# Transformed convolution with batch norm: loads as whole 128-row arrays, and a new order of the first jobs, products and weights

## The chip, the core and the metric

The kernel runs on one core of a Trainium2 chip. A core has a matrix engine (TensorE, PE in the profile; PEld is its weight load), a vector engine (VectorE, DVE), a scalar engine (ScalarE, ACT), a general engine (GpSimd, POOL) and a queue engine (SyncE, SP) that issues most DMA transfers. The memory beside the engines has 128 partitions; matrix products land in PSUM, which has 8 banks here called 0 to 7, and PE may write a bank again only when its last reader is done. The metric is the device time of one execution in microseconds (us), given as the median of several.

## The reference

A one-dimensional convolution with 3 taps over a sequence, then batch norm with given mean and variance, then SiLU. Batch is 2, sequence length 2048, 1024 channels in and out, all in bf16:

```python
xp = jnp.pad(x, ((0, 0), (P, P), (0, 0)))            # P = 1
y = sum(jnp.einsum('bsc,cd->bsd', xp[:, k:k + S, :], w[k]) for k in range(3))
inv_std = 1.0 / jnp.sqrt(var + 1e-5)
y = (y - mean) * (g * inv_std) + b
return jax.nn.silu(y)
```

## The kernel before

The convolution is done in a transformed domain: six outputs at a time come from eight products instead of eighteen. The sequence is cut into groups of six rows, 342 of them, each read as a window of eight rows. The work has four steps.

**Jobs: transform of x.** A load of x (`load_x`, L106) brings one batch (of 2) and one block of 128 input channels (of 8): 128 partitions, 16 windows of 128 rows; there are 16 such loads, of 512 KB. A job matmul (L241) multiplies one window, as stationary operand, with the matrix `rm`, which holds the eight points for 21 groups: 168 columns. 6, 6 and then 4 such matmuls make one job, so that a load of x gives three jobs and all of it 48 jobs and 256 matmuls. A job fills two banks, and ACT (L264) or DVE (L266) cast it to bf16 into `T_sb`. The last six groups of each batch are a "short" block: one load `xl` (L102) of 48 rows, eight small matmuls (L255), one cast.

**Weights.** For each block of 128 output channels (`dc`, 8 of them) the three taps W0, W2, W1 (in this order in memory) become eight transformed weights. Products 0 and 7 use W0 and W2 as they are; for the six others POOL makes a sum `e` (L134) for each of three pairs, out of multiples of the taps (POOL L126 or ACT L124), and from each sum two weights `u` (L147), by adding and subtracting W1 or its double. The first block's are made by `FirstWeights`: W0 and W2 are loaded first, W1 later, and steps are issued in a fixed order as soon as their inputs have been issued. Multiples named in the order string (`m2a`: multiple 2 on ACT) are made there, the others on POOL. The second block is made by `prepare_second`, later ones by `prepare_w`.

**Units: products and their combination.** A unit is one output block and one batch: eight products of eight matmuls (342 columns each, over the input blocks), in four banks, with copies, combinations on DVE (L309) and SiLU on ACT (L313). There are 16 units. In the first, products are issued one matmul at a time (L414): "ends" are products 0 and 7, which go to banks 2 and 3 and are copied out into `kept`; "p" are products 1 to 6. Later units use L294.

**Parameters.** `scales` on POOL (L216 to L225) turns variance, gain, mean and offset (`prm`) into a scale and an offset per output channel. It stands ahead of the first weights on POOL.

**What sets the order.** All engine queues are written out by hand, each engine runs its instructions in order, and SP's queue holds the loads in the order of the program: three loads of x, the short block, W0 and W2, the other loads of x (L106; each needs a free one of six buffers), W1, the second batch, its short block, the second block of weights. `rm` and `prm` go on ACT's queue. While x is transformed, the string `ORDER` says what PE does next: a letter A to D is one job, into banks 4, 6, 2 or 0 and the bank behind it, with `a`, `d` for the engine that casts it (two letters: one for each bank); `s2d` is a short block into bank 2, cast by DVE; a number is so many end products, `p` and a number so many of products 1 to 6; `+` is one waiting combination; `m2a` a multiple. Before it, PE runs three warm-up products on zeros (L87).

Of the kernel before, what the change touches and what calls it, by code (L numbers as in the profile page):

```python
# [8 lines left out]
ALU = mybir.AluOpType  # L9
FP32 = mybir.dt.float32  # L10
BF16 = mybir.dt.bfloat16
ENG = mybir.EngineType

P = 128
R = 6
NJ = 8
WT = 21
XBUFS = 6
LROWS = 48
SROW = 66  # L20
# [6 lines left out]

BANKS = {"A": 4, "B": 6, "C": 2, "D": 0}
ORDER = (
    "Bad Aad Da Cda Bda Ad Da Bda s2d Aad Dad Bad 2 Aa Dda 1 Bda Aad 1 Dad 1 Bda 1 Aa 1 Dda 1 Bda 1 Ada "  # L30
    "Dda Bad 1 m2a 2 Dd 2 Bda Aad Dda 2 Bad Aad p4 Ca p1 Bad p2 Aad Cda Ba p1 Ada p2 Ca p1 Bda p2 Aad p1 "
    "Ca p1 Bda p1 Aa p1 Cd p2 Bad p5 + Cad Ba p4 s4a Ca Bda Aa"
)

W0, W2, W1 = range(3)
COPIES = {0: "a", 7: "d", 1: "d", 3: "d", 2: "a", 5: "a"}

@with_exitstack
def kernel(
# [2 lines left out]
    x: bass.AP,  # L42
    xl: bass.AP,
    w: bass.AP,
    prm_in: bass.AP,
    rm_in: bass.AP,
    out: bass.AP,
):
    nc = tc.nc
    B, CT, _, NF, _ = x.shape  # L50
    DC = w.shape[0]
    NB = NTILES
    LAST = NB - NF * WT
# [22 lines left out]
    T_sb = [tpool.tile([P, CT, NJ, NB], BF16, name=f"T_sb{bi}") for bi in range(B)]  # L76


    rm = consts.tile([P, NJ, WT], BF16, name="rm")
    nc.scalar.dma_start(out=rm, in_=rm_in)  # L80
    prm = consts.tile([P, 4, DC], BF16, name="prm")


    zero = consts.tile([P, 1], FP32, name="zero")
    nc.gpsimd.memset(zero, 0.0)
    for n in (384, 384, 216):
        nc.tensor.matmul(  # L87
            ps[:, 3, 0:n], lhsT=zero.broadcast_to([P, P]), rhs=zero.broadcast_to([P, n]), start=True, stop=True,
        )
    zeros = consts.tile([P, 64], FP32, name="zeros")  # L90
    nc.vector.memset(zeros, 0.0)
# [12 lines left out]
    def load_x(bi, ct):  # L104
        xt[bi, ct] = t = xpool.tile([P, NF, P], BF16, name="xw")
# [26 lines left out]
    def even(dc, q, a, b):  # L132
        sums[dc, q] = epool.tile([P, CT, P], FP32, name=f"e{q}")
        nc.gpsimd.tensor_tensor(sums[dc, q], a, b, op=ALU.add)  # L134
# [29 lines left out]
    class FirstWeights:  # L164
# [3 lines left out]
        def __init__(self, dc):  # L168
            w0, w2 = raw[dc][:, W0], raw[dc][:, W2]
            self.dc, self.src, self.made = dc, ((w2, 4.0), (w0, 4.0), (raw[dc][:, W1], 2.0)), {}  # L170
            elsewhere = [int(t[1]) for t in ORDER.split() if t[0] == "m"]
            self.steps = [(None, lambda: even(dc, 0, w0, w2))]
            self.steps += [(i, lambda i=i: self.multiple(i, nc.gpsimd)) for i in (0,) if i not in elsewhere]
            self.steps += [(0, lambda: even(dc, 1, self.made[0], w0))]
            self.steps += [(i, lambda i=i: self.multiple(i, nc.gpsimd)) for i in (1,) if i not in elsewhere]
            self.steps += [(1, lambda: even(dc, 2, self.made[1], w2))]
            self.steps += [(i, lambda i=i: self.multiple(i, nc.gpsimd)) for i in (2,) if i not in elsewhere]
            self.steps += [
                (2 if q else None, lambda q=q, i=i: transform_w(dc, q, (i,)))
                for q, i in ((0, 0), (1, 0), (0, 1), (1, 1), (2, 0), (2, 1))  # L180
            ]
# [32 lines left out]
    beta = consts.tile([P, DC], FP32, name="beta")  # L214

    def scales():  # L216
        mhalf = consts.tile([P, DC], FP32, name="mhalf")
        nc.gpsimd.memset(mhalf, -0.5)
        sc = consts.tile([P, DC], FP32, name="sc")
        nc.gpsimd.tensor_scalar(sc, prm[:, 0, :], 1e-5, 1.0, op0=ALU.add, op1=ALU.mult)  # L220
        nc.gpsimd.tensor_tensor(sc, sc, mhalf, op=ALU.pow)
# [3 lines left out]
        nc.gpsimd.tensor_scalar(scale, sc, 1.0 / 36.0, 0.0, op0=ALU.mult, op1=ALU.add)  # L225
# [3 lines left out]
    class Jobs:  # L229
# [20 lines left out]
        def do_short(self, bank, eng):  # L250
            bi = self.short.pop(0)
            src = ps[:, bank, 0:CT * NJ * LAST].rearrange("p (c j n) -> p c j n", j=NJ, n=LAST)
            rows, n = (slice(0, P), SROW // R) if bi else (slice(0, LROWS), 0)
            for c in range(CT):
                nc.tensor.matmul(  # L255
                    src[:, c], lhsT=small[rows, c * P:(c + 1) * P], rhs=rm[rows, :, n:n + LAST],
                    start=True, stop=True,
                )
            dst = T_sb[bi][:, :, :, NT:NB].rearrange("p c j n -> p (c j) n")
            self.out(dst, src.rearrange("p c j n -> p (c j) n"), eng)  # L260
# [127 lines left out]
    class First(Unit):  # L388
# [3 lines left out]
        def __init__(self, dc, bi):  # L392
            super().__init__(dc, bi, 0)
            self.sd = dpool.tile([P, 4, NB], FP32, name="sd")
            self.t = [
                consts.tile([P, 2, NB], FP32, name="f0"), ypool2.tile([P, 2, NB], FP32, name="t1"),
                consts.tile([P, 2, NB], FP32, name="f2"),
            ]
            self.kept = consts.tile([P, 2, NB], FP32, name="kept")
            self.ends = [(j, q, False, ct) for ct in range(CT) for j, q in ((0, 2), (NJ - 1, 3))]  # L400
            self.todo = [
                (j, q, add, ct) for j, q, add in (
                    (1, 1, False), (3, 0, False), (2, 1, True), (4, 0, True), (5, 2, False), (6, 2, True),
                ) for ct in range(CT)
            ]
            self.p, self.later = {}, []
# [128 lines left out]

    nc.scalar.dma_start(out=prm, in_=prm_in)
    for ct in range(3):
        load_x(0, ct)  # L540
    load_small(0)
    load_w(0, slice(W0, W1))
    scales()
    nc.scalar.activation(dummy[:, 1:2], dummy[:, 0:1], ACT.Silu)
    for ct in range(3, CT):
        load_x(0, ct)
    load_w(0, slice(W1, W1 + 1))
    for ct in range(CT):
        load_x(1, ct)
    load_small(1)  # L550
# [7 lines left out]
    for token in ORDER.split():  # L558
# [49 lines left out]
    inner, outer = slice(2, R), slice(0, 2)  # L608
    h0 = Half(dc, bi, 4, 0)

    nc.tensor.matmul(ps[:, 5, 0:H], lhsT=zeros[:, 0:64].bitcast(BF16), rhs=T_sb[bi][:, 0, 0, 0:H], start=True, stop=True)  # L611
    h0.run(quiet, prev.rest(quiet, 5, 5))
    prev.store(nc.sync)
    h1 = Half(dc, bi, 0, 1)
# [21 lines left out]
def _laid_out(np, x, w, mean, var, g, b):  # L636


    B, S, C = x.shape
    K, _, D = w.shape  # L640
    CT, DC = C // P, D // P
    NF = S // (R * WT)
    step = R * WT
    xp = np.zeros((B, step * NF + P, C), x.dtype)
    xp[:, 1:S + 1] = x
    wins = np.stack([xp[:, f * step:f * step + P] for f in range(NF)], 2)
    wins = wins.reshape(B, P, NF, CT, P).transpose(0, 3, 1, 2, 4)
# [40 lines left out]
```

## Time and profile before

| | |
|---|---|
| median of 3 runs | 180.94 us (180.89 to 181.15) |
| profiled execution | 180.88 us, its span 179.1 us |
| PE busy | 172.7 us, 96% of the span |
| POOL busy | 139.7 us, 78% |
| DVE busy | 147.6 us, 82% |
| ACT busy | 110.2 us, 62% |
| chain that ended last | PE 86%, DMA 8%, DVE 3%, ACT 1% |
| DMA | 24.58 MB, mean 137 GB/s over the span |

The chain is followed back from the last instruction. Its DMA share, 8%, lies in the first 19 us, where x comes in; from there to about 170 us it is PE alone, and at the end the last unit's combinations and stores. So the table of averages says little on the head, and the prediction reads that part in order of time. In rows of the trace, a start and a length are in us from the start of the span; a bracket gives the idle time of the engine before it and what ended that; x and a number count instructions that the row merges.

### The profile page before, as it was taken

What the parts mean: (1) busy time and instruction counts of PE and PEld (TensorE: products, weight loads), DVE (VectorE), ACT (ScalarE), POOL (GpSimd) and SP (SyncE); (2) the same over time, 40 slices, a digit from 0 to 9 for tenths busy, and PEclk for the clock granted to TensorE, in tenths of its full rate; (3) what the DMA queues carried; (4) which work ended last, traced back from release to release, by engine and by line L of the source; (5) the groups of instructions that cost most, each with busy time, mean ns of one, the idle gap of its engine ahead of it and who ended that gap; (6) DMA issues with size and microseconds to landing.
All of it is one profiled execution on the core that took longest, in us unless ns stands there. A gap on an engine that the chain in (4) does not pass through costs nothing.

```text
span 179.1 us, 3534 instructions
## 1 busy us (share of the span) xinstructions
PE 172.7 (96%) x1367; PEld 123.5 (69%) x1367; DVE 147.6 (82%) x211; ACT 110.2 (62%) x191; POOL 139.7 (78%) x77
## 2 busy tenths in 40 slices
PE   8879999999999999999999999999999999999991
PEld 4869888766666666666666666666666666668891
DVE  1779998897969999997878788898979987766691
ACT  3779999959374837374636654565356554563774
POOL 2599999999997799999999999999799959000000
PEclk9999999999999999999999999999999999999999
DMA  5999993450344031813082306330303030203033
GB/s 187 374 410 404 410 383 124 129 226 0 132 141 170 0 132 8 260 45 132 0 221 90 134 0 168 143 134 0 135 0 132 0 130 6 98 34 132 3 149 117
DMA packets 6912, 24.58 MB, mean 137 GB/s; under 512 B 1040, under 2 KB 1552, under 8 KB 6896
## 3 DMA queue, kind: packets, MB, share of 16 engines
q1 hardware_dynamic: 6464, 24.25, 36.8%
q8 instruction: 10, 0.16, 0.3%
q10 hardware_dynamic: 432, 0.12, 0.3%
q14 instruction: 6, 0.05, 0.1%
HBM read 14.93 MB, written 9.44 MB: 136 GB/s over the span
## 4 chain that ended last, share of the span: by engine, by line
PE 86%; DMA 8%; DVE 3%; ACT 1%; SPq 0%; issue 0%; DVEq 0%
PE ps L294 75%; DMA xw<-in_x_dram 8%; PE ps L241 6%; PE ps L414 4%; DVE ps L309 2%; DVE t L309 1%; ACT yh L313 1%; SPq L106 0%; PE ps L255 0%; DVEq L677 0%; DVE sd L309 0%; PE ps L611 0%; DVEq L309 0%
## 5 line engine op out<-in xcount | busy, mean ns | idle before, releaser
L294 PE MATMUL ps<-T_sb,u 128*128 128x342 bf16 (+2 forms) x768 | 109.4, 298 | 0.0
L294 PEld LDWEIGHTS <-u 128*128 128x128 bf16 x768 | 72.3, 97 | 32.6
L147 POOL TENSOR_TENSOR u<-e,w1x 128x1024 bf16<-128x1024 f32 x32 | 71.5, 2258 | 6.1 <-DVE e L140 6.0
L294 PE MATMUL ps<-T_sb,wch 128*128 128x342 bf16 (+2 forms) x256 | 39.5, 299 | 0.4 <-DVE ps L309 0.4
L309 DVE SCALAR_TENSOR_TENSOR t<-ps,sd 128x684 f32<-128x684 f32 (+2 forms) x49 | 37.6, 819 | 0.5
L313 ACT ACTIVATE yT<-ps,beta,scale 128x342 bf16<-128x342 f32 (+1 forms) x42 | 29.2, 727 | 12.6 <-PE ps L294 12.6
L147 POOL TENSOR_TENSOR u<-e,wch 128x1024 bf16<-128x1024 f32 x16 | 35.7, 2251 | 0.5
L294 PEld LDWEIGHTS <-wch 128*128 128x128 bf16 x256 | 24.2, 97 | 11.1 <-issue 0.5
L303 ACT COPY pc<-ps 128x342 f32<-128x342 f32 (+2 forms) x32 | 13.6, 425 | 27.9 <-PE ps L294 27.0
L266 DVE CAST T_sb<-ps 128x504 bf16<-128x504 f32 (+3 forms) x37 | 22.8, 664 | 6.8 <-PE ps L241 6.3
L264 ACT CAST T_sb<-ps 128x504 bf16<-128x504 f32 (+4 forms) x46 | 25.5, 640 | 3.7 <-PE ps L241 3.6
L309 DVE SCALAR_TENSOR_TENSOR ps<-ps,t 128x684 f32<-128x684 f32 (+2 forms) x32 | 26.5, 829 | 0.7
L309 DVE SCALAR_TENSOR_TENSOR ps<-ps,pc 128x342 f32<-128x342 f32 (+2 forms) x34 | 16.9, 498 | 11.5 <-PE ps L294 8.8
L241 PE MATMUL ps<-rm,xw 128*128 128x168 bf16 x256 | 23.2, 236 | 1.8 <-DMA xw<-in_x_dram 1.6
L241 PEld LDWEIGHTS <-xw 128*128 128x128 bf16 x256 | 19.7, 98 | 4.8 <-DMA xw<-in_x_dram 2.9
L140 DVE SCALAR_TENSOR_TENSOR e<-wch 128x1024 f32<-128x1024 bf16 x12 | 21.0, 1749 | 0.0
L134 POOL TENSOR_TENSOR e<-wch 128x1024 f32<-128x1024 bf16 x8 | 19.0, 2374 | 0.1
L313 ACT ACTIVATE yT<-t,beta,scale 128x684 bf16<-128x684 f32 x15 | 14.4, 958 | 0.0
L309 DVE SCALAR_TENSOR_TENSOR sd<-pc,ps 128x342 f32<-128x342 f32 (+2 forms) x17 | 8.2, 485 | 7.4 <-ACT sd L303 7.4
L309 DVE SCALAR_TENSOR_TENSOR t<-ps,t 128x684 f32<-128x684 f32 (+2 forms) x17 | 13.9, 817 | 0.0
L303 ACT COPY sd<-ps 128x342 f32<-128x342 f32 (+2 forms) x16 | 6.8, 428 | 10.6 <-PE ps L294 8.9
L305 ACT ACTIVATE pc<-ps 128x342 f32<-128x342 f32 (+2 forms) x16 | 7.0, 438 | 8.7 <-PE ps L294 6.0
(44 smaller groups left out, 68.2 us busy)
## 6 DMA issues: line engine op xcount, KB each, us to landing
out_dram<-yT SPq DMA_DIRECT2D x15, 576.0 KB, 2.8
xw<-in_x_dram SPq DMA_DIRECT2D x16, 512.0 KB, 7.2
wch<-in_w_dram SPq DMA_DIRECT2D x7, 768.0 KB, 5.5
wch<-in_w_dram SPq DMA_DIRECT2D x1, 512.0 KB, 6.5
wch<-in_w_dram SPq DMA_DIRECT2D x1, 256.0 KB, 8.5
out_dram<-yh SPq DMA_DIRECT2D x1, 256.0 KB, 2.1
xl<-in_xl_dram SPq DMA_DIRECT2D x2, 96.0 KB, 5.9
out_dram<-yh SPq DMA_DIRECT2D x1, 128.0 KB, 1.7
```

Source lines behind the costliest of these rows:

```text
L134: nc.gpsimd.tensor_tensor(sums[dc, q], a, b, op=ALU.add)
L140: nc.vector.scalar_tensor_tensor(out=e, in0=f, scalar=4.0, in1=h, op0=ALU.mult, op1=ALU.add)
L147: nc.gpsimd.tensor_tensor(wts[dc, q][:, i], sums[dc, q], o, op=(ALU.add, ALU.subtract)[i])
L241: nc.tensor.matmul(src[:, q // per, q % per], lhsT=xt[bi, ct][:, f + q], rhs=rm, start=True, stop=True)
L264: nc.scalar.copy(dst, src)
L266: nc.vector.tensor_copy(dst, src)
L294: nc.tensor.matmul(self.bank[q], lhsT=lhsT, rhs=T_sb[self.bi][:, ct, j, nsl], start=not add and ct == 0, stop=ct == CT - 1, skip_group_che ...
L303: nc.scalar.copy(dst, self.bank[q])
L305: nc.scalar.mul(dst, self.bank[q], by)
L309: nc.vector.scalar_tensor_tensor(out=out, in0=in0, scalar=scalar, in1=in1, op0=ALU.mult, op1=op1)
L313: nc.scalar.activation(self.yT[:, rows, self.y0:self.y0 + self.hi - self.lo], src, ACT.Silu, bias=beta[:, dc:dc + 1], scale=scale[:, dc:dc ...
L414: nc.tensor.matmul(self.bank[q], lhsT=lhsT, rhs=T_sb[self.bi][:, ct, j, :], start=not add and ct == 0, stop=ct == CT - 1, skip_group_check ...
```

## The change

- `rm`, a copy of it for the short blocks, and `prm` become one array `head` with 128 rows, loaded in one transfer on ACT's queue.
- The short block of a batch is laid out by the host as 128 rows and three columns of 128 channels: three blocks of 40 rows stand above each other in a column, and the matrix for them is zero outside the 40 rows of its block. `small` becomes one tile for each batch, of 128 rows; the clearing of it goes. The eight short matmuls of a batch stay.
- W1 is loaded behind the fifth load of x instead of the eighth.
- `FirstWeights`: the two weights of a sum follow that sum, instead of all six behind the three sums. Multiple 1 goes to ACT (`m1a`); multiple 0 stays on POOL.
- The first unit's products run 1, 2, 3, 4, 5, 6 instead of 1, 3, 2, 4, 5, 6; one of its combinations goes (another takes its value from a neighbour), `kept` shares a tile with a result, and the copies of products 0 and 7 change engines.
- `ORDER` is another, with the first products ahead of the third load's last job.
- The warm-up is 24 columns shorter; the zero operands and -0.5 are taken from other tiles.

```diff
-LROWS = 48
-SROW = 66
+LROWS = 40
+STACK = 3
 ORDER = (
-    "Bad Aad Da Cda Bda Ad Da Bda s2d Aad Dad Bad 2 Aa Dda 1 Bda Aad 1 Dad 1 Bda 1 Aa 1 Dda 1 Bda 1 Ada "
-    "Dda Bad 1 m2a 2 Dd 2 Bda Aad Dda 2 Bad Aad p4 Ca p1 Bad p2 Aad Cda Ba p1 Ada p2 Ca p1 Bda p2 Aad p1 "
-    "Ca p1 Bda p1 Aa p1 Cd p2 Bad p5 + Cad Ba p4 s4a Ca Bda Aa"
+    "Dad Bad Aa Cda Bda Dd Aad s2a Ba 1 Dd 1 m1a 2 Aad Dad 1 Ba Ada 1 Dda 1 Bd 1 m2a Dda Ada 2 Bad Dda "
+    "Aad 2 Ba p5 Ada Bda p1 1 Ada p1 1 Bda 2 p1 Aad Ba Cda p4 Ada p1 Cad p3 + + Aad + p3 Ca p2 Bda p1 "
+    "Ada p2 Cad Ba Ada p2 Cda p1 Bda Ada Cda Bda p2 Aad p1 s3a Bda Ada Cda p1 Ba Aa"
 )
+COPIES = {0: "d", 7: "a", 1: "d", 3: "d", 2: "a", 5: "a"}
-COPIES = {0: "a", 7: "d", 1: "d", 3: "d", 2: "a", 5: "a"}
...
-    rm = consts.tile([P, NJ, WT], BF16, name="rm")
-    nc.scalar.dma_start(out=rm, in_=rm_in)
-    prm = consts.tile([P, 4, DC], BF16, name="prm")
+    ends = (0, NJ * WT, NJ * (WT + STACK * LAST))
+    first = consts.tile([P, head.shape[1]], BF16, name="head")
+    nc.scalar.dma_start(out=first, in_=head)
+    rm = first[:, :ends[1]].rearrange("p (j n) -> p j n", j=NJ)
+    rm_short = first[:, ends[1]:ends[2]].rearrange("p (s j n) -> p s j n", s=STACK, j=NJ)
+    prm = first[:, ends[2]:].rearrange("p (i d) -> p i d", i=4)
...
-    for n in (384, 384, 216):
+    for n in (384, 384, 192):
...
-    small = xlpool.tile([P, CT * P], BF16, name="xl")
-    nc.vector.memset(small, 0.0)
+    small = [xlpool.tile([P, xl.shape[2]], BF16, name=f"xl{bi}") for bi in range(B)]
     def load_small(bi):
-        nc.sync.dma_start(out=small[bi * SROW:bi * SROW + LROWS], in_=xl[bi])
+        nc.sync.dma_start(out=small[bi], in_=xl[bi])
...
-            self.steps = [(None, lambda: even(dc, 0, w0, w2))]
-            self.steps += [(i, lambda i=i: self.multiple(i, nc.gpsimd)) for i in (0,) if i not in elsewhere]
-            self.steps += [(0, lambda: even(dc, 1, self.made[0], w0))]
...
-                for q, i in ((0, 0), (1, 0), (0, 1), (1, 1), (2, 0), (2, 1))
-            ]
+            self.steps = [(None, lambda: even(dc, 0, w0, w2))] + weights(0)
+            self.steps += multiple(0) + [(0, lambda: even(dc, 1, self.made[0], w0))] + multiple(2) + weights(1)
+            self.steps += multiple(1) + [(1, lambda: even(dc, 2, self.made[1], w2))] + weights(2)
...
-                    src[:, c], lhsT=small[rows, c * P:(c + 1) * P], rhs=rm[rows, :, n:n + LAST],
+                    src[:, c], lhsT=small[bi][:, c // STACK * P:(c // STACK + 1) * P], rhs=rm_short[:, c % STACK],
...
-            self.kept = consts.tile([P, 2, NB], FP32, name="kept")
+            self.kept = self.t[2]
...
-                    (1, 1, False), (3, 0, False), (2, 1, True), (4, 0, True), (5, 2, False), (6, 2, True),
+                    (1, 1, False), (2, 1, True), (3, 0, False), (4, 0, True), (5, 2, False), (6, 2, True),
...
-            if j == 1:
-                self.combine(sd[:, 3], b1, 2.0, self.kept[:, 1])
...
-                    lambda: self.combine(sd[:, 3], sd[:, 3], 1.0, b1, ALU.subtract),
+                    lambda: self.combine(sd[:, 3], sd[:, 2], 1.0, self.kept[:, 1]),
...
-    nc.scalar.dma_start(out=prm, in_=prm_in)
     for ct in range(3):
         load_x(0, ct)
     load_small(0)
     load_w(0, slice(W0, W1))
+    for ct in range(3, 5):
+        load_x(0, ct)
+    load_w(0, slice(W1, W1 + 1))
     scales()
     nc.scalar.activation(dummy[:, 1:2], dummy[:, 0:1], ACT.Silu)
-    for ct in range(3, CT):
+    for ct in range(5, CT):
         load_x(0, ct)
-    load_w(0, slice(W1, W1 + 1))
...
-    while unit.todo[0][0] == 4:
+    while unit.todo[0][0] != 5:
```

More of the change, by code (lines that the diff above doesn't have):

```diff
@@ L18 @@
 XBUFS = 6
-LROWS = 48
-SROW = 66
+LROWS = 40
+STACK = 3
 NTILES = 342
+LAST = 6
 NBP = 384
@@ L44 @@
     w: bass.AP,
-    prm_in: bass.AP,
-    rm_in: bass.AP,
+    head: bass.AP,
     out: bass.AP,
@@ L52 @@
     NB = NTILES
-    LAST = NB - NF * WT
     NT = NF * WT
@@ L89 @@
         )
-    zeros = consts.tile([P, 64], FP32, name="zeros")
-    nc.vector.memset(zeros, 0.0)
     dummy = consts.tile([P, 2], FP32, name="dummy")
@@ L171, in __init__, with multiple, weights @@
             elsewhere = [int(t[1]) for t in ORDER.split() if t[0] == "m"]
-            self.steps = [(None, lambda: even(dc, 0, w0, w2))]
-            self.steps += [(i, lambda i=i: self.multiple(i, nc.gpsimd)) for i in (0,) if i not in elsewhere]
-            self.steps += [(0, lambda: even(dc, 1, self.made[0], w0))]
[L175 to L179, printed above, removed]
-                for q, i in ((0, 0), (1, 0), (0, 1), (1, 1), (2, 0), (2, 1))
-            ]
+            def multiple(i):
+                return [(i, lambda: self.multiple(i, nc.gpsimd))] if i not in elsewhere else []
+            def weights(q):
+                return [(2 if q else None, lambda i=i: transform_w(dc, q, (i,))) for i in (0, 1)]
+            self.steps = [(None, lambda: even(dc, 0, w0, w2))] + weights(0)
+            self.steps += multiple(0) + [(0, lambda: even(dc, 1, self.made[0], w0))] + multiple(2) + weights(1)
+            self.steps += multiple(1) + [(1, lambda: even(dc, 2, self.made[1], w2))] + weights(2)
             self.own = [i for i in range(3) if i not in elsewhere]
@@ L216, in scales @@
     def scales():
-        mhalf = consts.tile([P, DC], FP32, name="mhalf")
-        nc.gpsimd.memset(mhalf, -0.5)
+        nc.gpsimd.memset(scale, -0.5)
         sc = consts.tile([P, DC], FP32, name="sc")
         nc.gpsimd.tensor_scalar(sc, prm[:, 0, :], 1e-5, 1.0, op0=ALU.add, op1=ALU.mult)
-        nc.gpsimd.tensor_tensor(sc, sc, mhalf, op=ALU.pow)
+        nc.gpsimd.tensor_tensor(sc, sc, scale, op=ALU.pow)
         nc.gpsimd.tensor_tensor(sc, prm[:, 1, :], sc, op=ALU.mult)
@@ L252, in do_short @@
             src = ps[:, bank, 0:CT * NJ * LAST].rearrange("p (c j n) -> p c j n", j=NJ, n=LAST)
-            rows, n = (slice(0, P), SROW // R) if bi else (slice(0, LROWS), 0)
             for c in range(CT):
                 nc.tensor.matmul(
-                    src[:, c], lhsT=small[rows, c * P:(c + 1) * P], rhs=rm[rows, :, n:n + LAST],
+                    src[:, c], lhsT=small[bi][:, c // STACK * P:(c // STACK + 1) * P], rhs=rm_short[:, c % STACK],
                     start=True, stop=True,
@@ L609 @@
     h0 = Half(dc, bi, 4, 0)
-    nc.tensor.matmul(ps[:, 5, 0:H], lhsT=zeros[:, 0:64].bitcast(BF16), rhs=T_sb[bi][:, 0, 0, 0:H], start=True, stop=True)
+    nc.tensor.matmul(ps[:, 5, 0:H], lhsT=zero.bitcast(BF16)[:, 0:1].broadcast_to([P, P]), rhs=T_sb[bi][:, 0, 0, 0:H], start=True, stop=True)
     h0.run(quiet, prev.rest(quiet, 5, 5))
@@ L647, in _laid_out @@
     wins = wins.reshape(B, P, NF, CT, P).transpose(0, 3, 1, 2, 4)
-    rm = np.zeros((P, NJ, WT), np.float32)
+    rm, short = np.zeros((P, NJ, WT), np.float32), np.zeros((P, STACK, NJ, LAST), np.float32)
     for n in range(WT):
         rm[R * n:R * n + NJ, :, n] = np.array(_POINTS, np.float32).T
+    for s in range(STACK):
+        short[s * LROWS:(s + 1) * LROWS, s] = rm[:LROWS, :, :LAST]
+    prm = np.stack([var, g, mean, b]).reshape(4, DC, P).transpose(2, 0, 1)
+    xl = np.zeros((B, -(-CT // STACK), P, P), x.dtype)
+    for c in range(CT):
+        rows = slice(c % STACK * LROWS, (c % STACK + 1) * LROWS)
+        xl[:, c // STACK, rows] = xp[:, step * NF:step * NF + LROWS, c * P:(c + 1) * P]
     return (
         wins,
-        xp[:, step * NF:step * NF + LROWS],
+        xl.transpose(0, 2, 1, 3).reshape(B, P, -1),
         w[[0, 2, 1]].reshape(K, CT, P, DC, P).transpose(3, 2, 0, 1, 4),
-        np.stack([var, g, mean, b]).reshape(4, DC, P).transpose(2, 0, 1),
-        rm.astype(x.dtype),
+        np.concatenate([a.reshape(P, -1).astype(x.dtype) for a in (rm, short, prm)], 1),
     )
@@ L669 @@
     given = {k: _np.asarray(v) for k, v in inputs.items()}
-    for name, a in zip(("x", "xl", "w", "prm", "rm"), _laid_out(_np, **given)):
+    for name, a in zip(("x", "xl", "w", "head"), _laid_out(_np, **given)):
         a = _np.ascontiguousarray(a)
```

## The prediction

> **What bounds the kernel now.** I read the page's first part, then the waits of the matrix engine, then busy time by stage, then the head in order of time. First the page:
>
> ```profile
> span 179.1 us, 3534 instructions
> PE 172.7 (96%) x1367; PEld 123.5 (69%) x1367; DVE 147.6 (82%) x211; ACT 110.2 (62%) x191; POOL 139.7 (78%) x77
> ```
>
> The profiled execution took 180.88 us, so 1.78 us lie outside its span; the median of the runs, 180.94, is 0.06 above it. PE is busy 96%, so the rest is in few places. Busy time by stage (stage, its length, then PE, PEld, DVE, ACT, POOL; last columns clock, DMA share, GB/s):
>
> ```profile
> 4.70:9.30 4.60, 4.29 (x56) 3.67 (x55) 3.91 (x7) 3.79 (x7) 2.69 (x7) 1.00 1.04 379
> 9.30:18.63 9.33, 8.07 (x95) 7.09 (x95) 8.18 (x15) 8.35 (x17) 9.01 (x6) 1.00 1.03 406
> 18.63:36.68 18.05, 18.05 (x194) 15.15 (x195) 16.17 (x28) 16.97 (x31) 17.97 (x9) 1.00 0.71 263
> 36.68:170.20 133.52, 133.52 (x943) 90.80 (x941) 113.77 (x148) 74.73 (x126) 108.95 (x49) 1.00 0.26 91
> ```
>
> From 18.63 to 170.20 PE has no gap. Whatever the change gives lies ahead of 18.63, where the DMA engines are full (share 1.03, 406 GB/s), or it breaks the stretch behind. The waits name the loads of x:
>
> ```profile
> PE ps L241 <- DMA xw<-in_x_dram: 1.6, 3, 1.1
> ```
>
> In order of time (start, length, count; in brackets the idle time before):
>
> ```profile
> 4.71 2.53 PE L241 MATMUL ps<-rm,xw 128*128 128x168 bf16 x32 [0.19 <-DMA rm<-in_rm_dram]
> 7.52 1.04 PE L241 MATMUL ps<-rm,xw 128*128 128x168 bf16 x12 [0.28 <-DMA xw<-in_x_dram]
> 8.50 0.39 PE L255 MATMUL ps<-rm,xl 48*128 48x48 bf16 x8
> 8.81 0.46 PE L241 MATMUL ps<-rm,xw 128*128 128x168 bf16 x4
> 10.38 1.04 PE L241 MATMUL ps<-rm,xw 128*128 128x168 bf16 x12 [1.10 <-DMA xw<-in_x_dram]
> 11.26 0.45 PE L414 MATMUL ps<-T_sb,wch 128*128 128x342 bf16 x2
> 17.99 0.45 PE L414 MATMUL ps<-T_sb,wch 128*128 128x342 bf16 x2
> 18.63 1.33 PE L241 MATMUL ps<-rm,xw 128*128 128x168 bf16 x16 [0.18 <-DMA xw<-in_x_dram]
> 19.80 0.45 PE L414 MATMUL ps<-T_sb,wch 128*128 128x342 bf16 x2
> 20.09 1.03 PE L241 MATMUL ps<-rm,xw 128*128 128x168 bf16 x12
> 20.96 0.74 PE L414 MATMUL ps<-T_sb,u 128*128 128x342 bf16 x4
> ...
> 32.61 1.91 PE L414 MATMUL ps<-T_sb,u 128*128 128x342 bf16 x12
> 34.36 1.33 PE L294 MATMUL ps<-T_sb,u 128*128 128x342 bf16 x8
> ```
>
> A job matmul costs 72.5 ns (12 from 20.09 to 20.96), a product 145 ns (2 from 19.80 to 20.09). At 34.36 the first unit has only its last 8 products left. From 7.52 to 34.36 PE does 224 job matmuls (256 less the 32 of the first row), 56 products and 16 short ones: 224 x 0.0725 + 56 x 0.145 + 2 x 0.31 (8.50 to 8.81, taken for both) = 16.24 + 8.12 + 0.62 = 24.98 us in 26.84. So **1.86 us are waits**, most of them ahead of 10.38 and of 18.63. No instruction of PE is added or removed, so this is what can be won; the wait ahead of 7.52 is for the third load of x, which stays third.
>
> **The change part by part.** The loads first: the SP queue in order of time, then landings (KB, us from issue; one x load, the first weights' W0 and W2, their W1, and the spread over all x loads):
>
> ```profile
> 0.72 1.33 SPq L106 DMA_DIRECT2D xw<-in_x_dram  x3
> 2.57 0.42 SPq L111 DMA_DIRECT2D wch<-in_w_dram  x1
> 3.03 4.56 SPq L106 DMA_DIRECT2D xw<-in_x_dram  x5
> 7.65 0.42 SPq L111 DMA_DIRECT2D wch<-in_w_dram  x1
> ```
> ```profile
> wch<-in_w_dram SPq DMA_DIRECT2D x1, 512.0 KB, 6.5
> xw<-in_x_dram SPq DMA_DIRECT2D x1, 512.0 KB, 7.3
> wch<-in_w_dram SPq DMA_DIRECT2D x1, 256.0 KB, 8.5
> DMA to landing us min/median/max: 3.7/7.2/9.3
> ```
>
> W0 and W2 land at 2.57 + 6.5 = 9.07, the fourth x (issued 3.03) at 10.33, W1 at 16.15. At 406 GB/s a 512 KB load occupies 1.29 us, W1 0.65.
>
> *One array of matrices and parameters (head).* 88 KB instead of 42 and 8, one issue on ACT's queue fewer. PE started at 4.71 on rm. Lower bound: the 0.19 us ahead of 4.71 vanish; upper: the array lands as late as the parameters did (POOL's row 6.16 below). By the first PE starts at 4.5, by the second at 6.2; I take 4.8, next to rm, since it moves the same 128 rows. Late by up to 0.4 it is covered by the wait ahead of 7.52; at 6.2 the jobs of x loads 1 and 2 end at 6.2 + 32 x 0.0725 = 8.52, 1.0 late, of which the new waits at 9.12 and 10.38 below (0.81) take back nearly all. Cost 0, at worst 0.2.
>
> *Short blocks in three columns.* xl keeps its 96 KB, spread over 128 rows; still 8 short matmuls per batch. The memset of xl and one of zeros leave DVE before it has work. The second batch's load stays behind all x. Cost 0, bounds 0 and 0.1 (more, smaller rows).
>
> *W1 ahead of the sixth x.* W1 then lands at 10.33 + 1.29 (fifth x) + 0.65 = 12.27 instead of 16.15; x loads 6 to 8 come 0.65 later (13.56, 14.85, 16.14), later ones as before. In SP's queue the sixth x is passed by it, nothing else; issue takes 0.42 and the queue holds several us of backlog (7.2 us median to landing).
>
> *New order.* From 7.52, by the order string: job 7 (6 matmuls) to 7.96; short 0.31, to 8.27; job 8 (6) to 8.70; then a product, whose W0 lands at 9.07 and, with some 0.05 until PE moves, starts at 9.12: **wait 0.42**. That product, job 9 (4) and three products: 0.145 + 0.29 + 0.435, to 9.99; the fourth x lets PE go at 10.38 as before: **wait 0.39**. Then 32 job matmuls and 4 products, 2.32 + 0.58, to 13.28; the sixth x lands at 13.56: **wait 0.33**, to 13.61. From there each x is in before its jobs: the eighth is wanted at 13.61 + 32 x 0.0725 + 4 x 0.145 + 5 x 0.145 = 17.24 and lands at 16.14, the ninth is wanted near 19.0, and landed by 18.6 here. The sum of the new waits is 1.14 against 1.86.
>
> What hides a late job here is the product put before or behind it, but PE goes through both in order. In the rows above the two products at 11.26 stood behind the wait that ended at 10.38, though their weights had landed at 9.07. The Trainium skill says the same (TensorE: Matmul & The Clock Gate, Part 2): only weight loads are pulled ahead, matmuls stay in program order. That speaks against the change, which puts a product in wait for W0 ahead of job 9, whose x is there: by that rule the 0.42 us stand; were jobs let past, 0.29 of them would go and the sum be 0.29 better. By that rule the trace agrees: the wait at 10.38 held ready products.
>
> *POOL's order and the scale parameters.*
>
> ```profile
> 6.16 0.20 POOL L220 TENSOR_SCALAR sc<-prm 128x8 f32<-128x8 bf16 x1 [4.57 <-DMA prm<-in_prm_dram]
> 9.01 0.20 POOL L225 TENSOR_SCALAR scale<-sc 128x8 f32<-128x8 f32 x1
> 9.28 2.12 POOL L134 TENSOR_TENSOR e<-wch 128x1024 f32<-128x1024 bf16 x1
> 11.47 1.05 POOL L126 TENSOR_SCALAR w1x<-wch 128x1024 bf16<-128x1024 bf16 x1
> 24.27 6.33 POOL L147 TENSOR_TENSOR u<-e,w1x 128x1024 bf16<-128x1024 f32 x3
> 30.54 2.15 POOL L134 TENSOR_TENSOR e<-wch 128x1024 f32<-128x1024 bf16 x1
> 45.56 4.23 POOL L147 TENSOR_TENSOR u<-e,w1x 128x1024 bf16<-128x1024 f32 x2
> ```
> ```profile
> 48.29 1.33 PE L294 MATMUL ps<-T_sb,u 128*128 128x342 bf16 x8
> ```
>
> With the parameters near 4.8 the scales (6.16 to 9.21, 3.05 us) end at 7.9. The first sum then starts at 9.12 and ends at 11.31 (2.19, from 9.28 to 11.47). The two weights behind it wait for W1 at 12.27. From there six weights of 2.09 (three from 24.27 to 30.54), one multiple of 1.13, two sums of 2.2: 18.1, end 30.4, against 30.54: nearly the same, since the idle 1.0 replaces the multiple that goes to ACT. The first weights are ready at 14.4, the others at 16.5, 21.9, 24.0, 28.2, 30.4; by the walk PE wants them at 16.5, 21.0, 23.3, 26.8, 32.5, 34.8. All covered. Behind that the second channel block's chain runs on POOL without a break; its fifth weight is ready at 45.56 + 2.12 = 47.68 and used at 48.29: 0.61 to spare, and the forecast gain uses 0.55 of it. Cost 0, but this is the next limit.
>
> *Casts, copies and combines.* Means of the commonest casts, of a copy and of a multiple:
>
> ```profile
> L264 ACT CAST T_sb<-ps 128x504 bf16<-128x504 f32 x28 | 15.6, 601 | 3.1 <-PE ps L241 3.1
> L266 DVE CAST T_sb<-ps 128x504 bf16<-128x504 f32 x28 | 18.0, 678 | 6.5 <-PE ps L241 6.1 <-ACT T_sb L264 0.3
> L425 DVE TENSOR_SCALAR pc<-ps 128x342 f32<-128x342 f32 x2 | 1.0, 502 | 0.0
> 17.93 1.06 ACT L124 ACTIVATE w1x<-wch 128x1024 bf16<-128x1024 bf16 x1
> ```
>
> ACT gains one multiple, 1.06, and casts some 0.5 less; DVE casts some 1.1 more and drops one combine (0.5). ACT was idle 0.98 + 1.08 in the two middle stages, DVE 1.15 + 1.88. Less 0.55 of added work and 0.55 of shorter time, ACT keeps about 1.0, DVE 1.9. Product 2 now adds to product 1's bank directly behind it: its copy (0.50) has three jobs, 16 x 0.0725 = 1.16 us, as cover; without cover it would cost the copy and a cast ahead of it, 1.2. Followed bank by bank, casts end 0.05 to 0.4 ahead of the next use; a few will miss. I take 0.15, bounds 0 and 0.7.
>
> *Kept in another tile, zeros gone, shorter warm-up:* no path; the combine that now writes the kept tile follows its readers on the same engine. Cost 0.
>
> Sum: 1.86 - 1.14 - 0.15 = 0.57; the landings shift by some hundredths; I take **0.55**. Nothing behind 36.68 changes but its start: 180.88 - 0.55 = 180.33, by the median's 0.06 some 180.35.
>
> **The rivals.** *Evacuation takes it.* ACT's spare 1.0 us in 27 is spread over 48 jobs; each miss makes PE wait. For it: 94% busy after 18.63; against: banks are reused two or three jobs later. Misses of 0.4 to 1.0 give 180.6 to 181.2, say 180.8.
>
> *W1 late, slower.* All weights but the first sum now queue behind W1. If it lands d after 12.27, POOL's chain moves by d; spare to 48.29 is 0.61 + 0.14 - 0.55 = 0.2. From d = 0.75 the gain is gone, beyond it each us costs one. For it: one x load took 9.3 instead of 7.2, and PE's wait at 18.63 is that load. That lateness, 2.1, gives 180.35 + 1.9 = 182.25. Against: W1 landed in its turn here.
>
> *More is won.* The sixth x comes in time or the casts never hold: waits fall to about 0.8, gain 1.0, 179.9; POOL's limit of 0.75 then binds, so 180.1 unless the second block's weights come earlier.
>
> *The loads decide nothing:* what is won at 10.38 is given back at 13.61 and at later loads. Against: after 18.63 PE never waits for x. It gives 180.9.
>
> **How the numbers follow.** Forecast 0.50 (180.2 to 180.55); casts or loads take it 0.22 (180.6 to 181.2); W1 or another late feed 0.15 (above 181.2); more 0.13 (179.8 to 180.2). The measurement can tell 0.2%, 0.36 us, from no change: faster means below 180.58, slower above 181.30. Faster 0.50 x 0.96 + 0.13 + a little of the casts = 0.63; slower 0.15; same 0.22. The range 179.95 to 181.3 leaves out W1's case and a corner of the last. The likeliest's own range is 180.2 to 180.55.
>
> **What would show it.** Right: PE waits near 9.1 for wch and near 13.6 for xw; nothing over 0.2 behind; first products near 9.1; the unit's last eight begin near 33.7 to 33.8. POOL idle near 11.3 for W1, then none until dc 1 is done. Wrong: PE waiting for casts (L264, L266) after 14, for POOL near 47.7, or the array landing past 5.2.

## The result, and the profile after

The changed kernel takes 189.17 us (median, 188.37 to 189.63) against 180.91 (180.86 to 181.15) measured beside it: a ratio of 1.0449, with the interval 1.0405 to 1.0493. It is slower by 8.3 us, where a gain of 0.55 was forecast. The profiled execution took 188.72 us.

The page of the changed kernel, its first lines:

```profile
span 186.7 us, 3530 instructions
PE 174.5 (93%) x1367; PEld 124.5 (67%) x1367; DVE 152.1 (81%) x210; ACT 110.9 (59%) x193; POOL 137.6 (74%) x76
```

PE's busy time has grown by 1.8 us with no instruction added, and 5.8 more are idle. Busy time by stage, the same stages as before (stage, its length, then PE, PEld, DVE, ACT, POOL; last columns clock, DMA share, GB/s):

```profile
9.30:18.63 9.33, 5.96 (x65) 4.85 (x66) 6.29 (x10) 4.57 (x7) 7.86 (x5) 0.96 1.03 407
18.63:36.68 18.05, 14.77 (x148) 12.62 (x148) 11.31 (x22) 13.96 (x27) 12.15 (x6) 0.83 0.59 199
```

PE loses 2.11 us of busy time in the first of these stages (8.07 before) and 3.28 in the second (18.05 before), and in the second its clock is 0.83, where it was 1.00. The waits of the changed kernel (total, times, longest, us) show two that the kernel before does not have:

```profile
ACT w1x L123 <- POOL e L133: 6.4, 1, 6.4
PE ps L239 <- ACT T_sb L261: 6.1, 1, 6.1
```

In order of time, the three engines together:

```profile
12.73 4.20 POOL L146 TENSOR_TENSOR u<-e,wch 128x1024 bf16<-128x1024 f32 x2 [1.19 <-DMA wch<-in_w_dram]
15.09 0.67 PE L239 MATMUL ps<-head,xw 128*128 128x168 bf16 x7
17.02 1.05 POOL L125 TENSOR_SCALAR w1x<-wch 128x1024 bf16<-128x1024 bf16 x1
18.15 2.12 POOL L133 TENSOR_TENSOR e<-w1x,wch 128x1024 f32<-128x1024 bf16 x1
20.30 1.06 ACT L123 ACTIVATE w1x<-wch 128x1024 bf16<-128x1024 bf16 x1 [6.42 <-POOL e L133]
21.87 1.42 PE L239 MATMUL ps<-head,xw 128*128 128x168 bf16 x9 [6.12 <-ACT T_sb L261]
```

Read from the bottom. PE stands still for 6.12 us until 21.87: its next bank has not been cast. The cast is queued on ACT behind the multiple `m2a`, which starts at 20.30 after 6.42 us of waiting. `m2a` multiplies W1, which was in by 12.73, when POOL's first weights started on it, so it does not wait for data: it starts when POOL's second sum ends (18.15 + 2.12 = 20.27). That sum reads multiple 0 (`w1x` in the rows is the tile of the multiples). They lie in a rotating store of two buffers (`spool`, `bufs=2`, the function `scaled`); multiple 0 has one, `m1a` the other, and `m2a` is to be written over multiple 0. In the kernel before, the same sum ran here (timeline of before):

```profile
12.60 2.13 POOL L134 TENSOR_TENSOR e<-w1x,wch 128x1024 f32<-128x1024 bf16 x1
```

It ended at 14.73 and `m2a` started at 17.93: 3.2 us to spare. The change puts two weights, and their wait for W1, ahead of multiple 0, and makes the sum 5.5 us later.

The standstill also costs clock. Busy time by stretch (same columns), in the changed kernel:

```profile
18.00:20.00 2.00, 0.00 (x0) 0.00 (x0) 0.00 (x0) 0.00 (x0) 1.92 (x2) 0.50 1.01 403
21.80:24.60 2.80, 2.73 (x17) 2.32 (x17) 0.68 (x1) 1.96 (x6) 2.80 (x2) 0.50 0.00 0
24.70:26.00 1.30, 1.30 (x17) 1.13 (x15) 0.35 (x1) 0.69 (x2) 1.30 (x2) 1.00 0.42 76
```
```profile
25.16 1.03 PE L239 MATMUL ps<-head,xw 128*128 128x168 bf16 x12
```

The granted clock is 0.50 from about 17.8, still inside the gap, until about 24.65. From the restart at 21.87 to the row at 25.16 PE does 13 job matmuls and 7 products. That takes 3.29 us; at 72.5 and 145 ns each it would be 1.96, so the half clock costs about 1.3 us. The Trainium skill (TensorE: Matmul & The Clock Gate, Part 1) says that after an idle window of about 3.4 us the gate passes half the pulses. The trace agrees that a long gap halves the clock, but here it halved about 2.1 us after the last matmul's end (15.76), sooner than a whole such window; it was full again 2.8 us after the restart. Standstill and half clock are about 7.4 us; where the second unit began (34.36 before), it begins 7.8 later:

```profile
42.13 1.32 PE L291 MATMUL ps<-T_sb,u 128*128 128x342 bf16 x8
```

(The prediction took the row at 34.36 for the first unit's last eight products; those are the next eight, 35.52 before and 43.29 here. The shift is the same.) The whole loss is made ahead of this.

### The profile page after: what moved, and what is told of

It is laid out like the page before. It is cut to its first block, busy times and chain, and to the rows that moved or that the text cites. A ratio compares the mean times of both kernels' runs of the same rounds, so it can differ in the third digit from the quotient of the medians.

```text
span 186.7 us, 3530 instructions
## 1 busy us (share of the span) xinstructions
PE 174.5 (93%) x1367; PEld 124.5 (67%) x1367; DVE 152.1 (81%) x210; ACT 110.9 (59%) x193; POOL 137.6 (74%) x76
## 4 chain that ended last, share of the span: by engine, by line
PE 82%; DMA 6%; POOL 4%; DVE 4%; issue 1%; ACT 1%; DVEq 0%; POOLq 0%
PE ps L291 72%; PE ps L239 6%; DMA wch<-in_w_dram 4%; PE ps L412 4%; POOL u L146 2%; DMA head<-in_head_dram 2%; DVE ps L306 2%; POOL e L133 1%; DVE T_sb L263 1%; DVE t L306 1%; POOL w1x L125 1%; ACT yh L310 1%; ACT T_sb L261 0%; DVEq L680 0%; DVE sd L306 0%
## 5 line engine op out<-in xcount | busy, mean ns | idle before, releaser
L146 POOL TENSOR_TENSOR u<-e,w1x 128x1024 bf16<-128x1024 f32 x32 | 69.4, 2194 | 8.8 <-DVE e L139 6.2
L146 POOL TENSOR_TENSOR u<-e,wch 128x1024 bf16<-128x1024 f32 x16 | 36.5, 2304 | 1.7 <-DMA wch<-in_w_dram 1.2
L263 DVE CAST T_sb<-ps 128x504 bf16<-128x504 f32 (+2 forms) x39 | 23.5, 658 | 14.0 <-PE ps L239 13.9
L239 PE MATMUL ps<-head,xw 128*128 128x168 bf16 x256 | 24.4, 241 | 7.5 <-ACT T_sb L261 6.1
L239 PEld LDWEIGHTS <-xw 128*128 128x128 bf16 x256 | 20.4, 100 | 11.2 <-issue 6.4
L306 DVE SCALAR_TENSOR_TENSOR ps<-ps,t 128x684 f32<-128x684 f32 (+2 forms) x32 | 26.5, 829 | 0.7
L139 DVE SCALAR_TENSOR_TENSOR e<-wch 128x1024 f32<-128x1024 bf16 x12 | 26.7, 2221 | 0.0
L123 ACT ACTIVATE w1x<-wch 128x1024 bf16<-128x1024 bf16 x11 | 11.6, 1053 | 6.4 <-POOL e L133 6.4
```

The source lines that it names most:

```text
L123: nc.scalar.mul(t, src, by)
L139: nc.vector.scalar_tensor_tensor(out=e, in0=f, scalar=4.0, in1=h, op0=ALU.mult, op1=ALU.add)
L146: nc.gpsimd.tensor_tensor(wts[dc, q][:, i], sums[dc, q], o, op=(ALU.add, ALU.subtract)[i])
L239: nc.tensor.matmul(src[:, q // per, q % per], lhsT=xt[bi, ct][:, f + q], rhs=rm, start=True, stop=True)
L263: nc.vector.tensor_copy(dst, src)
L306: nc.vector.scalar_tensor_tensor(out=out, in0=in0, scalar=scalar, in1=in1, op0=ALU.mult, op1=op1)
```

## The experiments

My theory: the second buffer's reuse is the cause, and with a third one the forecast 180.35 comes out. Rival A: the load of W1 and POOL's late weights hold PE anyway, so that a third buffer gives little. Rival B: the casts on ACT are too many in this order.

**A third buffer for the multiples (`e1`).** The changed kernel, with

```diff
-    spool = ctx.enter_context(tc.tile_pool(name="spool", bufs=2))
+    spool = ctx.enter_context(tc.tile_pool(name="spool", bufs=3))
```

> The changed kernel with three buffers instead of two for the multiples of the taps (tile w1x2), nothing else. Theory, reuse of the buffer: multiple 2 on ACT waits for the second sum on POOL because it takes the buffer of multiple 0, and every cast behind it on ACT waits too. Then the gap of PE from 15.8 to 21.9 and the half clock behind it vanish, and the head goes as in the prediction: 180.3 us (180.0 to 180.9). Rival, W1 or POOL's order as such makes ACT wait: time stays within 1 us of 189.2.

Measured: 181.81 us (181.41 to 181.97), ratio 1.0036 (1.0025 to 1.0047). 7.36 of the 8.26 us are gone. Stages and timeline of this kernel; `m2a` (13.34, on ACT) no longer waits:

```profile
9.30:18.63 9.33, 8.65 (x98) 7.08 (x97) 7.43 (x12) 8.43 (x15) 7.98 (x5) 1.00 1.03 408
18.63:36.68 18.05, 17.44 (x189) 14.56 (x188) 17.36 (x32) 16.44 (x32) 17.81 (x9) 1.00 0.61 230
```
```profile
8.98 0.32 PE L412 MATMUL ps<-T_sb,wch 128*128 128x342 bf16 x1 [0.28 <-DMA wch<-in_w_dram]
10.27 1.04 PE L239 MATMUL ps<-head,xw 128*128 128x168 bf16 x12 [0.25 <-DMA xw<-in_x_dram]
13.34 1.08 ACT L123 ACTIVATE w1x<-wch 128x1024 bf16<-128x1024 bf16 x1
13.51 1.04 PE L239 MATMUL ps<-head,xw 128*128 128x168 bf16 x12 [0.17 <-DMA xw<-in_x_dram]
16.42 0.89 PE L412 MATMUL ps<-T_sb,u 128*128 128x342 bf16 x5
17.58 1.04 PE L239 MATMUL ps<-head,xw 128*128 128x168 bf16 x12 [0.27 <-DMA xw<-in_x_dram]
24.13 2.13 POOL L133 TENSOR_TENSOR e<-w1x,wch 128x1024 f32<-128x1024 bf16 x1
25.45 1.18 DVE L306 SCALAR_TENSOR_TENSOR sd<-sd,f 128x342 f32<-128x342 f32 x1
26.34 2.27 POOL L146 TENSOR_TENSOR u<-e,w1x 128x1024 bf16<-128x1024 f32 x1
27.10 1.11 PE L239 MATMUL ps<-head,xw 128*128 128x168 bf16 x9 [0.42 <-DVE T_sb L263]
```

The clock is 1.00 and the long wait is gone, so both A and B fall as causes of the 8.3 us. (A bracket is the engine's idle time, less than the wait where matmuls overlap; from the last useful step to the next start the waits at 8.98, 10.27, 13.51 and 17.58 are 0.45, 0.41, 0.33 and 0.43.) But 0.75 us remain against before (181.06 in the same series), and 181.81 is outside what the theory expected. Two things were not forecast: the wait for the eighth load of x at 17.58, and waits for casts at 26.5 (0.58) and 27.4 (0.30), behind a combination that took 1.18 us instead of 0.50.

**The same buffer in the kernel before (`c1`).** The kernel before, with three buffers, and `self.kept = self.t[2]` in place of its own tile, to make room.

> The kernel before with three buffers for the multiples, and, for room, the copies of products 0 and 7 in the tile of a result as in the changed kernel. Theory: nothing there waits for that buffer, since the second sum ends at 14.8 and multiple 2 comes to ACT's turn at 17.9: 180.9, within 0.2%. Rival, a third buffer helps either kernel: faster by over 0.2%.

Measured: 181.16 us, ratio 1.0005 (0.9996 to 1.0013). In the old order the third buffer buys nothing: order and buffer count make the wait together.

**Two buffers, but POOL's second sum ahead of the weights (`e2`).** In `FirstWeights` of the changed kernel:

```diff
-            self.steps = [(None, lambda: even(dc, 0, w0, w2))] + weights(0)
-            self.steps += multiple(0) + [(0, lambda: even(dc, 1, self.made[0], w0))] + multiple(2) + weights(1)
+            self.steps = [(None, lambda: even(dc, 0, w0, w2))]
+            self.steps += multiple(0) + [(0, lambda: even(dc, 1, self.made[0], w0))] + weights(0) + multiple(2) + weights(1)
```

> The changed kernel with two buffers, but on POOL multiple 0 and the second sum stand ahead of the first two weights. Theory, reuse of the buffer: the second sum then ends near 14.9 instead of 20.3, multiple 2 waits about 1.4 us instead of 6.4, the first weights come near 17.0 and PE waits for them some 0.5: 181.0 to 182.0. Rival, the wait is for W1's late use or for casts: still over 186.

Measured: 182.73 us (182.3 to 183.23), ratio 1.0092 (1.0074 to 1.011), 0.7 above the range that was expected; but the long wait shrinks as its releaser moves, and the time with it. Its timeline:

```profile
14.35 1.06 ACT L123 ACTIVATE w1x<-wch 128x1024 bf16<-128x1024 bf16 x1 [1.01 <-POOL e L133]
15.93 0.86 PE L239 MATMUL ps<-head,xw 128*128 128x168 bf16 x9 [0.70 <-ACT T_sb L261]
```

`m2a` waits 1.01 us instead of 6.42 and PE 0.7 instead of 6.12: the wait follows the end of the sum. Of the time above the range, part is a later wait of PE for a cast (0.66 at 27.80), behind the same slow combination as in `e1`, here 1.43 us.

**The gap filled with work that counts for nothing (`e3`).** What does the half clock cost by itself? The changed kernel, with 28 additional matmuls on W0 into bank 0, which holds nothing then, ahead of the job that waits:

```diff
+FILL, NFILL = 29, 28
...
-    for token in ORDER.split():
+    for at, token in enumerate(ORDER.split()):
+        if at == FILL:
+            for _ in range(NFILL):
+                nc.tensor.matmul(ps[:, 0, 0:504], lhsT=raw[0][:, W0, 0], rhs=raw[0][:, W0, 0:4].rearrange("p c n -> p (c n)")[:, 0:504], start=True, stop=True)
```

> The changed kernel with 28 matmuls of 504 columns on W0 into a bank that the next job overwrites, put into PE's queue where its gap is; their results are not used. They take about 5.9 us at full clock, so PE stays busy through the gap, and the wait of ACT is untouched. Theory, the idle time lowers the granted clock: from 21.9 to 24.7 PE then runs at full clock and 1.4 us are won, 187.5 to 188.0. Rival, the lower clock has another cause or costs nothing: 189.2, or more if the added matmuls run into the work behind.

Measured: 187.57 us (187.21 to 188.53), 1.6 us below the changed kernel. Stretches of this kernel:

```profile
15.20:21.20 6.00, 6.00 (x32) 2.79 (x30) 0.80 (x2) 1.06 (x2) 4.74 (x3) 1.00 0.86 341
21.20:25.00 3.80, 3.62 (x38) 2.93 (x37) 2.05 (x4) 3.40 (x8) 3.73 (x2) 1.00 0.19 40
```

With PE busy through the gap the clock stays 1.00, and the same 13 job matmuls and 7 products take 2.13 us (21.71 to 23.84) instead of 3.29. So the price of the clock is 1.2 us by the two traces and 1.6 by the medians, of four runs each that spread over 1.3; the rest of the 7.4 is that of the standstill.

**The 0.75 us that remain: the combination (`f1`, `f2`).** The changed kernel replaces a combination of the fourth output, made from PSUM in two steps, by one that reads two tiles in SBUF (`sd<-sd,f`), while POOL works there too. `f1` is `e1` with the two steps of the kernel before; `f2` is `e1` with the short form left, but issued later, behind the next casts:

```diff
+            if j == 1:
+                self.combine(sd[:, 3], b1, 2.0, self.kept[:, 1])
...
-                    lambda: self.combine(sd[:, 3], sd[:, 2], 1.0, self.kept[:, 1]),
+                    lambda: self.combine(sd[:, 3], sd[:, 3], 1.0, b1, ALU.subtract),
```
```diff
...
-p3 + + Aad + p3
+p3 + + Aad p3
...
```

> e1_third_buffer with the first unit's fourth combination in its old form, two steps that each read product 1 or 2 from PSUM, instead of one step with all operands in SBUF. In e1_third_buffer that one step took 1.18 us where its neighbours take 0.50, and PE waited for casts at 26.5 and 27.3, 0.9 us together. Theory, all operands in SBUF are slow on DVE while POOL works: the two steps take 0.5 each, the waits fall to 0.3 or less, 0.5 to 0.8 faster than e1_third_buffer: 181.0 to 181.3. Rival, the order of casts is too tight there whatever the step takes: within 0.2 of 181.8.

> e1_third_buffer with that same step left in its SBUF form but moved behind the last cast, to the others that wait for product 4. Theory: it takes 1.2 us there too, or near it, but no cast stands behind it, so PE loses nothing: 0.5 to 0.9 faster than e1_third_buffer. Rival, the waits at 26.5 have another cause: they stay.

Measured: `f1` 181.45 us (181.03 to 181.97), ratio 1.0023 (1.0012 to 1.0034), a smaller gain than expected; `f2` 180.90 (180.28 to 181.47), ratio 0.9993 (0.9981 to 1.0006). In `f1` the combination takes 0.50 us and the waits for casts are gone, but the added step costs elsewhere (timeline of `f1`: product 2 waits 0.39 us in all for it):

```profile
21.32 0.50 DVE L306 SCALAR_TENSOR_TENSOR sd<-ps,f 128x342 f32<-128x342 f32 x1
21.88 0.74 PE L412 MATMUL ps<-T_sb,u 128*128 128x342 bf16 x4 [0.22 <-DVE sd L306]
```

In `f2` the slow combination is no faster, but it has no cast behind it that PE waits for (timeline and stage of `f2`):

```profile
32.73 4.49 POOL L146 TENSOR_TENSOR u<-e,wch 128x1024 bf16<-128x1024 f32 x2
33.06 2.17 DVE L306 SCALAR_TENSOR_TENSOR sd<-sd,f 128x342 f32<-128x342 f32 x1
```
```profile
18.63:36.68 18.05, 18.05 (x195) 15.07 (x194) 17.48 (x31) 16.98 (x34) 17.82 (x9) 1.00 0.67 250
```

PE is busy throughout the stage, and the 0.9 us between `e1` and `f2` (0.8 by the ratios) come from this step's place.

**What that step costs by itself (`g3`).** `e1`, with four additional combinations of tiles in SBUF at each of two places, one beside POOL's work and one behind its end; what they write is not used.

```diff
+    spare = unit.t
...
+        if i in (9, len(seq) - 2):
+            for _ in range(4):
+                unit.combine(spare[0][:, 0], spare[0][:, 1], 1.0, spare[2][:, 0])
```

> e1_third_buffer with eight more combinations of 342 columns with all operands in SBUF, on tiles that are free by then: four behind unit 9, near 105 us, where POOL works without a break, four behind unit 14, near 150 us, where POOL is done. Their results are not used. Theory, such a step waits for the running POOL instruction: near 150 us each takes 0.50, near 105 us the first takes up to 2.2 and POOL's instruction beside them grows. Rival, the step is slow by itself or by DVE's queue: the same length at both places.

A single run took 186.72 us; only its durations are used here (timeline; the first row shows three of the four steps):

```profile
121.69 7.15 DVE L306 SCALAR_TENSOR_TENSOR f<-f,f 128x342 f32<-128x342 f32 x3
126.07 2.40 POOL L146 TENSOR_TENSOR u<-e,w1x 128x1024 bf16<-128x1024 f32 x1
171.97 2.15 DVE L306 SCALAR_TENSOR_TENSOR f<-f,f 128x342 f32<-128x342 f32 x4
```

Beside POOL each of the four takes 2.3 to 2.4 us, one for each POOL instruction; with POOL done, 0.51 to 0.52.

**The loads alone (`f3`).** The changed loads (one array, three columns, W1 behind the fifth x) under the old `ORDER`, `COPIES`, steps of `FirstWeights` and combinations.

```diff
-    "Dad Bad Aa Cda Bda Dd Aad s2a Ba 1 Dd 1 m1a 2 Aad Dad 1 Ba Ada 1 Dda 1 Bd 1 m2a Dda Ada 2 Bad Dda "
...
+    "Bad Aad Da Cda Bda Ad Da Bda s2d Aad Dad Bad 2 Aa Dda 1 Bda Aad 1 Dad 1 Bda 1 Aa 1 Dda 1 Bda 1 Ada "
...
```

> The kernel before with the changed loads alone: one array of matrices and parameters, short blocks in three columns, W1 ahead of the sixth x, the old order of jobs, products and weights. Theory: the first two cost nothing; the sixth to eighth x come 0.65 later, PE waits some 0.3 near 13.3 and up to 1 near 16.4 where the load of PE's own code (16 KB on one of the 16 DMA engines) now falls on the eighth x, and the old wait of 0.4 near 18.6 goes: 181.3 to 182.2. Rival, loads cost nothing in the old order: 181.0, within 0.2%.

Measured: 180.88 us (180.4 to 181.7), ratio 0.9993 (0.9979 to 1.0006). My expectation of a loss missed. No cost and no gain of the loads can be told: PE's waits are others (0.99 for the fourth x as before, 0.31 for the sixth, none at 18.6) and the sum comes out the same.

```profile
10.22 1.04 PE L239 MATMUL ps<-head,xw 128*128 128x168 bf16 x12 [0.83 <-DMA xw<-in_x_dram]
```

**What delays the eighth load of x (`f5`).** In `e1` a 16 KB packet of queue q8, kind "instruction", runs at 15.2 us for 1.1 us on one of the 16 DMA engines, and the x load in flight lands late: the eighth is issued at 7.46 and lands 10.1 us later, at 17.53, 2.8 us behind the seventh, where the other loads of x near it land 1.28 apart. If the two belong together, 32 tiny matmuls more in the warm-up shift both:

```diff
+    for n in range(32):
+        nc.tensor.matmul(
+            ps[:, 3, 0:8], lhsT=zero.bitcast(BF16)[:, 0:1].broadcast_to([P, P]), rhs=zero.bitcast(BF16)[:, 0:1].broadcast_to([P, 8]), start=True, stop=True,
+        )
```

> e1_third_buffer with 32 matmuls of 8 columns more in the warm-up; their results are not used. They bring PE's code load, which comes when PE has started some 129 matmuls, forward by 32 of them. Theory, that load delays one DMA engine by 1.2 us and so the x load that is in flight: it then falls near 13 instead of 16, the wait of 0.33 for the sixth or seventh x grows to 1 or more, and the wait of 0.43 for the eighth x near 17.2 goes; time within 1 us of e1_third_buffer. Rival, the eighth x is late for another reason: its landing stays at 17.5.

Measured: 181.83 us (181.4 to 182.37), ratio 1.0044 (1.0031 to 1.0057), against `e1`'s 181.81. The packet runs at 12.06, and the wait goes from the eighth x to the sixth, which lands at 14.38 instead of 13.47 in `e1` (timeline of `f5`; PE stands from 13.2 to 14.42); the eighth lands at 16.94, 1.28 behind the seventh:

```profile
14.42 1.04 PE L243 MATMUL ps<-head,xw 128*128 128x168 bf16 x12 [1.05 <-DMA xw<-in_x_dram]
```

So the fetch of PE's instructions delays the load it meets. The other traces agree: in each, behind the fifth load of x, one load of x lands 1.9 to 2.8 us behind the load before it, the others 1.1 to 1.3, and the late one is in flight at the packet. In `f3`, with the packet at 15.37, it is the ninth (18.32, the eighth at 15.96), which PE does not want before 18.45, so no wait followed. In the kernel before, with the packet at 15.80, it is also the ninth (18.58), and PE's wait at 18.63 is for it. Why the packet at about 15.3 meets the eighth load in `e1`, `f2` and `g1` and the ninth in `e2`, `f3` and `g2` is open.

**Two attempts at a better version (`g1`, `g2`).** `g1` is `f2` and `g2` is `f1`, each with one more product 1 to 6 moved ahead of the job at the eighth x; in `g2` ACT copies product 0, too.

```diff
...
-p5 Ada Bda p1 1 Ada
+p6 Ada Bda 1 Ada
...
-COPIES = {0: "d", 7: "a", 1: "d", 3: "d", 2: "a", 5: "a"}
+COPIES = {0: "a", 7: "a", 1: "d", 3: "d", 2: "a", 5: "a"}
```

> f2_late_combine with six instead of five matmuls of product 1 ahead of the eighth x, where PE waited 0.42 for it. Theory: that wait shrinks by one product, 0.145, when it is there, and nothing else moves: 180.75, some 0.15 faster than f2_late_combine. Rival, the wait is not for the eighth x alone or the product's input is late: no change.

> f1_psum_combine with the copy of product 0 on ACT instead of DVE, and the sixth product matmul as in g1_late_combine_six. In f1_psum_combine PE waited 0.39 at 21.4 for the extra step of DVE ahead of product 2. Theory: with one copy less ahead of it DVE is done in time, the 0.39 go and up to 0.145 more: 180.9 to 181.1. Rival, ACT has no room for the copy and PE waits for casts instead: 181.4 or more.

Measured: `g1` 180.92 us (180.28 to 181.53), ratio 0.9991 (0.998 to 1.0002); `g2` 181.69 (181.17 to 181.98), ratio 1.0037 (1.0024 to 1.0049). Neither gain came: `g1` cannot be told from before or from `f2`, though PE no longer waits for the eighth x in its trace, and `g2` is above its range, where its rival had it; product 2 still waits 0.33 us for DVE, and why its median is above `f1`'s is open. No version beats the kernel before by more than the measurement can tell.

## Why the prediction was wrong

*Casts, copies and combines* is the step that failed, together with *POOL's order*, which put the moved sum at no cost. The first costed ACT's multiples by their 1.06 us alone; the second asked when POOL's outputs are ready, but not which engine waits until POOL has read its inputs. Neither asked which buffer `m2a` takes and who reads it last. The question "what is queued behind the waiting instruction" had an answer here: all of ACT's casts, hence PE's banks, hence PE. The row of `m2a` at 17.93 was quoted; the sum that frees its buffer, 3.2 us ahead, was in the same trace, and by the prediction's own walk the sum was to move behind two weights that wait for W1 at 12.27: 12.27 + 2 x 2.09 + 1.13 + 2.2 = 19.8, against 20.27 measured. The numbers for the loss were at hand. No rival held it. "Slower" was tied to W1 or another load landing late, and W1 hardly was: POOL's wait for it ended at 12.73, 0.5 behind the forecast. One of the prediction's own signs of being wrong, PE waiting for casts after 14, is what the trace shows, with 6.12 us.

With the third buffer the other steps can be read, in `e1`:

- *New order*: the waits forecast were 0.42, 0.39 and 0.33; measured 0.45, 0.41 and 0.33. Products stand behind a wait in program order, as argued. The walk to the first `p5` gave 16.51; measured 16.42. Missed: 0.43 us for the eighth x, forecast to land at 16.14 and landed at 17.53, which `f5` ties to the instruction fetch. It takes most of the forecast gain. The fetch could be seen ahead: the load that the prediction quotes with 9.3 us to landing instead of 7.2 is the one that the packet meets in the kernel before.
- *Casts, copies and combines*, apart from the buffer: taken 0.15, bounds 0 and 0.7; measured 0.9 between `e1` and `f2`. The cause is not the number of casts but one combination that POOL slows down; of this exchange the prediction counted only the combination that goes, 0.5 on DVE.
- *POOL's order*: the weights came within 0.3 us of the forecast, the last at 30.7 (forecast 30.4); PE never waits for them in `e1`.
- *One array*, *three columns*: cost 0, and `f3`, with the changed place of W1, shows none that can be told. The gain forecast from the loads and the order is not there even in `f2`, which has neither the buffer's wait nor the slow combination in PE's way: 0.9993 (0.9981 to 1.0006). In its profile the waits for W0, the fourth, sixth and eighth x add up to 1.6 us, as much as the kernel before waits at 10.38 and 18.63 (the prediction's 1.86 is all that its sum over matmuls left). That is the rival *The loads decide nothing*, at its 180.9.

## What to carry to other kernels

When the order of producers changes, follow each output tile to its buffer: in a rotating store, the new instruction waits for the last reader of the tile that held the buffer before, and that wait appears in no list of data dependencies. Price the wait at the engine's whole queue behind it, and add the clock if PE stands long enough to lose it (1.2 to 1.6 us here, after a gap of 6). Where a change frees memory, ask at once whether a store with few buffers can use it: one more buffer was worth 7.4 us here, and nothing where the order did not need it.

## What was not expected of the hardware

- A small DVE step with both inputs in SBUF takes 0.50 to 0.52 us alone and 1.2 to 2.4 beside POOL's sums and weights of 2.1 us; the DVE step ends some 0.4 us behind the end of the POOL instruction that ran when it began (26.26 and 26.63 in `e1`), and POOL's next takes 2.27 to 2.40 instead of 2.1. The same step with one input in PSUM took 0.50 beside POOL (`f1`). The Trainium skill (SBUF — State Buffer, Who interferes with whom) says that a DVE instruction with two SBUF inputs contends with a GpSimd instruction that reads SBUF, and that one with at most one SBUF input, outside certain fast modes, does not; the trace agrees with both.
- A fetch of 16 KB of PE instructions occupies one of 16 DMA engines for 1.1 us, and comes earlier when more instructions are issued before it (15.2 us in `e1`, 12.06 with 32 matmuls more). The load it meets lands 0.6 to 1.5 us later than at the usual distance of 1.28, and PE waits where it wants that load: 0.43 us in `e1`, 1.2 in `f5` (0.33 without the fetch).
- The kernels with the new loads scatter more (180.3 to 181.7) than the kernel before (180.85 to 181.6 over 33 runs, nearly all within 0.3). PE's early pace varies from run to run: job matmuls of 348 ns until about 5.6 us in the profiled execution of `f2`, 236 from 5 us on in `f1`, with the granted clock shown as 1.00 in both. Whether that is the cause, or which load the fetch meets, and which part of the new loads brings it, was not tried.
